# Half-precision Strassen sums with a power-of-two scale found on the chip, and one packed DRAM block per weight group

## The chip, the cores and the metric

The kernel runs on one core of one Trainium2 chip. The metric is device time in microseconds (us), the median of several executions. One execution of each kernel is also profiled; its trace gives the start, the duration and the releasing event of every instruction. TensorE is called PE, its weight loads PEld, VectorE DVE, ScalarE ACT, GpSimd POOL, SyncE SP. An engine name followed by q (ACTq, SPq, POOLq) is that engine's sequencer issuing a DMA.

Executions are fast or slow (over 1.5% above the fastest of the same kernel).

## The reference, cut to what matters

The input is 2048 tokens of width 1024 in bfloat16. The kernel does layernorm, linear attention with 32 heads, and a SwiGLU feed-forward block of width 3584:

```python
xn = layernorm(x)
s  = attention(xn, wqkv, wo)             # linear attention, phi(q), phi(k)
g  = silu((silu(xn @ w_gate) * (xn @ w_up)) @ w_down)
return x + s * g
```

The two large products `xn @ w_gate` and `xn @ w_up` are the subject. `w_gate` and `w_up` are 1024 x 3584 each.

## The kernel before

The kernel has these stages, in order: K and V projections; Q, attention and output projection (called "Q to S" below); the feed-forward block for one half of the tokens (gate/up, then down); and the same for the other half. I call the two gate/up stages pass 0 and pass 1.

Gate and up are computed by Strassen-Winograd. The weights are cut in 28 groups of 1024 x 256 (14 gate, 14 up). A group is a 2 x 2 block matrix; seven products of blocks replace eight. Three of them use the weights as they are, four use sums of weight blocks, T1 to T4, and of activation blocks, S1 to S4. Each product is four matmuls of 128x128 by 128x512, so a group is 28 matmuls. POOL makes the T sums once, in fp32, and keeps a copy in DRAM, which pass 1 (and part of pass 0) loads back:

```python
def t_pair():
    return [tp.tile([P, 2, HK, P], F32R, name="T%d" % k, tag="T") for k in range(2)]

def emit_T(key, w):
    b11, b12 = w[:, 0:HK, 0:P], w[:, 0:HK, P:2 * P]
    b21, b22 = w[:, HK:DC, 0:P], w[:, HK:DC, P:2 * P]
    ...
    nc.gpsimd.tensor_tensor(out=T1, in0=b12, in1=b11, op=ALU.subtract)
    nc.gpsimd.tensor_tensor(out=T2, in0=b22, in1=T1, op=ALU.subtract)
    nc.gpsimd.tensor_tensor(out=T3, in0=b22, in1=b12, op=ALU.subtract)
    nc.gpsimd.tensor_tensor(out=T4, in0=b21, in1=T2, op=ALU.subtract)
    ...   # first time: t_drams[g] <- ta, tb  (two fp32 tiles of 512 KB)

def emit_Ssum(p):
    ...
    S1, S2, S3, A22 = [sp.tile([P, HK, TB], F32R, ...) for k in range(4)]
    S4 = sp.tile([P, HK, TB], F16, name="S4", tag="S4")

def emit_a(key):           # four of the seven products of a group
    ...
    prod(y_[:], lambda k: T2[:, k, :], lambda k: S2[:, k, :], True)
    prod(x_[:], lambda k: w[:, k, 0:P], lambda k: x1[:, k, :], True)
    prod(zw[:, 0, :], lambda k: T3[:, k, :], lambda k: S3[:, k, :], True)
    prod(zw[:, 1, :], lambda k: T1[:, k, :], lambda k: S1[:, k, :], True)
    nc.scalar.copy(out=s1[:], in_=x_[:])                     # PSUM leaves through ACT and DVE
    nc.vector.tensor_tensor(out=s2[:], in0=y_[:], in1=s1[:], op=ALU.add)
```

Fourteen of the 28 groups are prepared during K/V and Q to S; the others arrive raw in pass 0 and are summed there. ACT both evicts PSUM for PE and issues DMAs.

## Time and profile before

The median is 803.16 us (802.13 to 803.51, three runs). First the page of the profiled execution of the kernel before, its engine line and its chain of work (what the end of the program depended on, followed back) as shares of the span:

```profile
PE 790.2 (99%) x3787; PEld 431.3 (54%) x3787; DVE 453.0 (57%) x739; ACT 232.9 (29%) x384; POOL 215.5 (27%) x357
...
PE 96%; DVE 2%; ACT 0%; DMA 0%; issue 0%; DVEq 0%; ACTq 0%
```

PE is busy for 99% of the 799.1 us span, and 96% of the chain is PE. So nothing else can be made faster with profit. The next lines are groups of PE instructions of the kernel before; the columns are line, engine, operation, output<-inputs, partitions x elements, type and count, then busy us and mean ns of one, then idle time before them:

```profile
L641 PE MATMUL zw<-S,T 128*128 128x512 f32 x672 | 175.3, 409 | 0.0
...
L641 PEld LDWEIGHTS zw<-S,T 128*128 128x128 f32 x672 | 126.4, 188 | 32.3
...
L641 PEld LDWEIGHTS <-w_sb 128*128 128x128 bf16 x672 | 56.8, 98 | 83.1 <-issue 30.5
```

A weight load of fp32 type takes 188 ns, one of 16-bit type 98 ns. The pitch of the groups shows in the timeline of PE (start, duration, what). Two neighbouring groups of pass 1 in the kernel before:

```profile
652.05 3.12 PE L641 MATMUL zw<-S,T 128*128 128x512 f32 x12
...
658.37 3.12 PE L641 MATMUL zw<-S,T 128*128 128x512 f32 x12
```

They start 6.32 us apart, 225.7 ns per matmul. Stages with only 16-bit matmuls run at 215.8 ns. That is the room the change aims at.

### The profile page before, as it was taken

Reading aid. Unit: us, or ns where it says so; the run is one execution under the profiler, and the core shown is the slowest. Engines: PE = TensorE matmul, PEld = TensorE weight load, DVE = VectorE, ACT = ScalarE, POOL = GpSimd, SP = SyncE. Lnnn points to the kernel's source line nnn. Section 1 sums busy time; section 2 is a strip of 40 time slices with the busy share of each in tenths; the row PEclk is TensorE's granted clock in tenths of the full one; section 3 lists DMA queues with packets and bytes.
Section 4 is the critical chain, followed back from the end, with each engine's and each line's share of the span. In section 5 each row is a group of like instructions: output and inputs, shape, how many; then the busy total and the mean of one; then the engine's idle time right before and its main releaser. Section 6 shows DMA issues by size and latency. Waiting matters only on the chain.

```text
span 799.1 us, 10159 instructions
## 1 busy us (share of the span) xinstructions
PE 790.2 (99%) x3787; PEld 431.3 (54%) x3787; DVE 453.0 (57%) x739; ACT 232.9 (29%) x384; POOL 215.5 (27%) x357
## 2 busy tenths in 40 slices
PE   8999999999999999999999999999999999999997
PEld 3544444554445666666664444466666666544443
DVE  7787344774575767677672071366767667601305
ACT  4544334866534222222220030122222232200102
POOL 0576799055005443535710020100000000000100
PEclk9999999999999999999999999999999999999999
DMA  9378974386478778787786457499777787744641
GB/s 321 114 175 172 300 260 187 103 207 191 133 168 275 235 244 266 230 270 232 224 304 218 151 188 284 129 324 310 239 251 253 256 251 251 253 169 137 232 131 53
DMA packets 155296, 173.68 MB, mean 217 GB/s; under 512 B 35440, under 2 KB 114672, under 8 KB 155248
## 3 DMA queue, kind: packets, MB, share of 16 engines
q1 hardware_dynamic: 143584, 136.20, 55.9%
q0 software_dynamic: 9216, 32.51, 11.5%
q10 hardware_dynamic: 2448, 4.33, 1.6%
q8 instruction: 30, 0.49, 0.2%
q14 instruction: 18, 0.15, 0.1%
HBM read 127.93 MB, written 37.75 MB: 207 GB/s over the span
## 4 chain that ended last, share of the span: by engine, by line
PE 96%; DVE 2%; ACT 0%; DMA 0%; issue 0%; DVEq 0%; ACTq 0%
PE zw L641 26%; PE kv_ps L402 13%; PE xb L641 12%; PE y_pd L726 12%; PE y_ps L726 11%; PE s_ps L578 7%; PE q_ps L158 7%; PE yb L641 7%; PE nd_ps L551 1%; PE kvz L424 1%; DVE sy L763 1%; DVE stats L321 0%; DVE io L764 0%; DMA xp<-in_A_x_dram 0%; PE tr_ps L386 0%
## 5 line engine op out<-in xcount | busy, mean ns | idle before, releaser
L641 PE MATMUL zw<-S,T 128*128 128x512 f32 x672 | 175.3, 409 | 0.0
L726 PEld LDWEIGHTS <-hT 128*128 128x128 bf16 x896 | 87.7, 98 | 105.7
L641 PEld LDWEIGHTS zw<-S,T 128*128 128x128 f32 x672 | 126.4, 188 | 32.3
L641 PE MATMUL xb<-xnT,w_sb 128*128 128x512 bf16 x448 | 115.2, 380 | 0.0
L402 PE MATMUL kv_ps<-wkv_sb,xnT 128*128 128x512 bf16 x512 | 113.6, 379 | 0.7 <-ACT r_t L139 0.5
L726 PE MATMUL y_ps<-w_sb,hT 128*128 128x512 bf16 x448 | 103.2, 379 | 0.0
L726 PE MATMUL y_pd<-w_sb,hT 128*128 128x512 bf16 x448 | 102.9, 379 | 0.0
L766 POOL DMA_DIRECT2D out_dram<-io x24 | 13.0, 540 | 332.6 <-DVE io L764 332.6
L641 PEld LDWEIGHTS <-w_sb 128*128 128x128 bf16 x672 | 56.8, 98 | 83.1 <-issue 30.5
L763 DVE TENSOR_TENSOR sy<-sy,io 128x512 f32<-128x512 f32 (+1 forms) x33 | 22.2, 672 | 137.6 <-ACT sy L762 137.4
L402 PEld LDWEIGHTS <-xnT 128*128 128x128 bf16 x512 | 49.3, 98 | 57.2 <-issue 0.7
L660 ACT COPY s<-xb 128x512 f32<-128x512 f32 x56 | 32.7, 584 | 158.4 <-PE xb L641 158.4
L214 POOL TENSOR_TENSOR T<-w_sb 128x512 fp32r<-128x512 bf16 x28 | 33.0, 1178 | 154.8 <-DMA w_sb<-in_B_w_up_dram 87.2
L661 DVE TENSOR_TENSOR s<-yb,s 128x512 f32<-128x512 f32 x56 | 38.6, 688 | 61.9 <-ACT s L660 61.9
L641 PE MATMUL yb<-S,T 128*128 128x512 f32 x224 | 71.5, 441 | 0.0
L158 PE MATMUL q_ps<-xnT,wq_sb 128*128 128x512 bf16 x256 | 58.2, 379 | 0.0
L698 ACT ACTIVATE sg<-sg 128x1024 f32<-128x1024 f32 x28 | 29.6, 1058 | 97.6 <-DVE sg L694 97.6
L641 PE MATMUL zw<-S,w_sb 128*128 128x512 f16 x224 | 58.0, 382 | 0.0
L578 PE MATMUL s_ps<-wo_sb,oT 128*128 128x512 bf16 x256 | 57.8, 379 | 0.0
L762 ACT ACTIVATE sy<-y_pd 128x512 f32<-128x512 f32 x16 | 8.7, 595 | 159.9 <-PE y_pd L726 159.9
L662 DVE TENSOR_TENSOR s<-zw,s 128x512 f32<-128x512 f32 x56 | 38.7, 692 | 26.6 <-PE zw L641 26.5
L704 DVE TENSOR_TENSOR hT<-cu,sg 128x1536 bf16<-128x1536 f32 x28 | 49.9, 1781 | 0.0
(84 smaller groups left out, 808.3 us busy)
## 6 DMA issues: line engine op xcount, KB each, us to landing
w_sb<-in_B_w_down_dram SPq DMA_DIRECT2D x56, 512.0 KB, 4.0
T<-t_g SPq DMA_DIRECT2D x52, 512.0 KB, 4.3
w_sb<-in_B_w_gate_dram SPq DMA_DIRECT2D x40, 512.0 KB, 4.8
t_g<-T POOLq DMA_DIRECT2D x28, 512.0 KB, 4.8
w_sb<-in_B_w_up_dram SPq DMA_DIRECT2D x28, 512.0 KB, 6.6
t_u<-T POOLq DMA_DIRECT2D x28, 512.0 KB, 4.8
T<-t_u SPq DMA_DIRECT2D x28, 512.0 KB, 4.8
s_dram<-s_sb ACTq DMA_DIRECT2D x16, 256.0 KB, 4.1
```

The costliest lines, as they stand in the source:

```text
L158: nc.tensor.matmul(q_ps[:], lhsT=wq_sb[:, dc, g * P:(g + 1) * P], rhs=xn_ap(dc, btok), start=(dc == 0), stop=(dc == DC - 1))
L214: nc.gpsimd.tensor_tensor(out=T1, in0=b12, in1=b11, op=ALU.subtract)
L402: mm = nc.tensor.matmul(kv_ps[:], lhsT=xn_ap(dc, tok), rhs=wkv_sb[:, dc, c * CW:(c + 1) * CW], start=(dc == 0), stop=(dc == DC - 1))
L578: mm = nc.tensor.matmul(s_ps[:], lhsT=oT[:, c, ttok], rhs=wo_sb[:, c, cc * CW:(cc + 1) * CW], start=(c == 0), stop=(c == G - 1))
L641: nc.tensor.matmul(out, lhsT=lhs(k), rhs=rhs(k), start=(first and k == 0), stop=(k == HK - 1), skip_group_check=True)
L660: nc.scalar.copy(out=s1[:], in_=x_[:])
L661: nc.vector.tensor_tensor(out=s2[:], in0=y_[:], in1=s1[:], op=ALU.add)
L662: nc.vector.tensor_tensor(out=s3[:], in0=zw[:, 0, :], in1=s2[:], op=ALU.add)
L698: nc.scalar.activation(out=c[:, 1:3, :], in_=c[:, 1:3, :], func=ACT.Silu)
L704: nc.vector.tensor_tensor(out=hv[:, TB:4 * TB], in0=c[:, 1:4, :].rearrange("p a b -> p (a b)"), in1=sg[:, 1:4, :].rearrange("p a b -> p (a ...
L726: nc.tensor.matmul(ys[(t, c)], lhsT=h[:, fc, tt], rhs=wt[:, o:o + CW], start=(fc == 0), stop=(fc == FC - 1), skip_group_check=True)
L763: nc.vector.tensor_tensor(out=sy[:], in0=sy[:], in1=s_in[:, cs], op=ALU.mult)
```

## The change

The intent is to make all gate/up matmuls 16-bit. Sums of weights in fp16 could overflow or underflow for other weights, so every group is first scaled by an exact power of two, found on the chip from the sum of the absolute weights; the inverse scale is applied where PSUM is evicted. Raw weights, scaled, and their four sums go into one 1 MB block per group, so that pass 1 loads one block. The core of the diff, with cuts:

```diff
-    wgu = ctx.enter_context(tc.tile_pool(name="wgu", bufs=3))
-    tp = ctx.enter_context(tc.tile_pool(name="tp", bufs=8))
+    wgu = ctx.enter_context(tc.tile_pool(name="wgu", bufs=NPK))      # 7 slots of 1 MB
+    stp = ctx.enter_context(tc.tile_pool(name="stp", bufs=4))
...
+    def emit_st0(key, t):
+        asum = stp.tile([P, 1], FP32, name="asum", tag="asum")
+        nc.scalar.activation(out=t[:, 1]..., in_=t[:, 0]..., func=ACT.Abs, accum_out=asum[:])
+        sd = dram.tile([P, 1], FP32, name="sd_%s%d" % key[1:])
+        nc.scalar.dma_start(out=sd[:], in_=asum[:])
+        st_tiles[key] = sd
+
+    def emit_st1(key):
+        sd = st_tiles.pop(key)
+        bc = stp.tile([P, P], FP32, name="bc", tag="bc")
+        nc.scalar.dma_start(out=bc[:], in_=sd[:].rearrange("p o -> (o p)").partition_broadcast(P))
+        st_tiles[key] = bc
+
+    def emit_st2(key, t):
+        bc = st_tiles.pop(key)
+        ...
+        nc.vector.tensor_reduce(out=tot[:], in_=bc[:], op=ALU.add, axis=mybir.AxisListType.X)
+        ...                                     # exponent of the total -> scale cs, inverse rc
+        nc.vector.tensor_scalar(out=w, in0=w, scalar1=cs_all[:, c:c + 1], scalar2=None, op0=ALU.mult)
...
     def emit_T(key, t):
...
+        pk = dram.tile([P, 2, DC, FW], BF16, name="pk_%s%d" % key[1:])
+        nc.gpsimd.dma_start(out=pk[:], in_=t[:])
...
-        emit_phi(phiw, q_ps[:], pqT[:, g, :], TB, in_place=True, act=b > 0 or g % 2 == 1)
+        emit_phi(phiw, q_ps[:], pqT[:, g, :], TB, in_place=True, act=b > 0)
...
-            nc.scalar.copy(out=s1[:], in_=x_[:])
-            nc.vector.tensor_tensor(out=s2[:], in0=y_[:], in1=s1[:], op=ALU.add)
+            nc.scalar.activation(out=s1[:], in_=x_[:], func=ACT.Copy, scale=rc)
+            nc.vector.scalar_tensor_tensor(out=s2[:], in0=y_[:], scalar=rc, in1=s1[:], op0=ALU.mult, op1=ALU.add)
...
-                io = tp.tile([P, 2, D], BF16, name="io", tag="T")
+                io = iop.tile([P, 2, D], BF16, name="io", tag="io")     # 2 buffers instead of 8
```

`asum` is one number per partition. To get the total onto all partitions, the change stores the 128 numbers to DRAM (128 rows of 4 bytes: 512 bytes in all) and loads them back as one row, broadcast to 128 partitions. I call this store and load the trip. `emit_st0`, `emit_st1` and `emit_st2` of one group run in three successive steps, so each engine has other work between them. In pass 0 a raw group is loaded six groups ahead, summed five ahead, scaled three ahead and used one ahead.

## The prediction

> **What bounds the kernel now.** TensorE. The page's engine table gives PE 790.2 us of a 799.1 us span, the chain of waits is 96% PE, and the list of PE's waits sums to about 4 us, all before 129 us. So time can only come from the pitch of the matmuls.
>
> **Pitch, from the PE timeline.** In the K/V, Q and down stages 32 bf16 matmuls start 6.90 us apart: 215.8 ns each (the Trainium skill, TensorE: Matmul & The Clock Gate, "Back-to-back issue gap", has about 216). In the gate/up stage each group of 28 matmuls takes 6.32 us: 225.7 ns each, the same in every group of both passes, so a rate and not a wait. 16 have fp32 operands; their weight loads take 188 ns against 98 ns for bf16 (groups by form). The same page ("Weight-path perf modes") says that fast weight load is off for FP32; the trace agrees with the factor of two.
>
> **What the change removes.** All gate/up matmuls become 16-bit. 784 matmuls per pass at 215.8 instead of 226 ns is 169.2 instead of 177.2 us: -8.0 us per pass, **-15.9 us** in all. This lies wholly on the critical path. Fewer bytes moved, faster Strassen sums and a bf16 hT product (1.78 to about 0.9 us) are off it and save nothing.
>
> **What it adds.** Per weight group (28, once each): a 2048-wide abs-sum on ACT (about 1.95 us), two small DMAs through DRAM (about 2 us each), five DVE operations (about 1.3 us). Where they bite:
> - Pass 0 of gate/up: ACT and DVE have room (DVE 120 us of 178). The chain for an unprepared group ends on POOL: scale done about 2.2 us after its predecessor's group, T1 and T2 2.4 us later, needed at 6.04 us. Slack about 1.4 us; the three raw groups at the end may cost some tenths. +0.5 us, and +0.5 at the start of the pass.
> - Q/attention stage (129 to 175 us): ACT was busy 15.6 of 18 us and DVE 15.9 of 18 us there. Q block 0 now goes wholly through DVE (two ops, 1.35 us per 1.73 us of PE) plus the mask products plus scaling, then block 1 wholly through ACT plus abs-sums. Summing durations in program order, DVE falls some 4 us behind and PE waits for PSUM: **+2.5 us** (1 to 5).
> - Tail: the output staging has 2 buffers instead of 8, so in the last sweep the loads of x and s for token tile 2 wait for tile 0's store. I expect **+2 us** (1 to 3.5) after the last matmul.
>
> **Predicted:** 803.2 - 15.9 + 1 + 2.5 + 2 = about **792 us** (-1.4%); 8 in 10 between 787.5 and 799. Faster by over 2%: 0.07; within 2%: 0.87; slower: 0.06.
>
> **What would show it.** Gate/up groups 6.04 us apart in both passes, weight loads 98 ns there; PE waits on DVE between 140 and 180 us; last matmul to end of span about 7 us instead of 5; no PE waits in the down stages or in pass 1.
>
> **What would make it wrong.** POOL slower on fp16 output or blocked by DVE: 14 unprepared groups, each with 1.4 us of slack, could give back up to 10 us. ACT stuck on a DMA semaphore in its fixed order, stopping evictions of PSUM, in the prep stretch (85 to 175 us). If all additions were hidden, 787.3 us, just on the 2% line.

## The result, and the profile after

The kernel became slower: 896.01 us (892.45 to 908.0, four runs, of which the one of 908.0 counts as slow and is left out of the ratio) against 802.64 us for the kernel before in the same session. Ratios in this document are the mean time of one kernel's fast runs over that of the other's of the same rounds, so they are not quite the ratio of the medians quoted; here it is 1.1149, with a 95% interval of 1.1121 to 1.1176.

The page of the changed kernel, the same two lines, and the chain by line:

```profile
PE 798.3 (89%) x3787; PEld 363.4 (41%) x3787; DVE 482.9 (54%) x883; ACT 283.8 (32%) x430; POOL 196.6 (22%) x329
...
PE 57%; DMA 23%; POOL 6%; DVE 5%; issue 4%; ACT 3%; ACTq 0%; SPq 0%; POOLq 0%; DVEq 0%
PE zw L681 14%; PE y_pd L777 11%; PE y_ps L777 10%; DMA sd_u<-asum 8%; PE xb L681 7%; PE s_ps L616 6%; DMA sd_g<-asum 6%; PE yb L681 4%; DMA bc<-sd_g 3%; PE q_ps L162 3%; DMA w_sb<-in_B_w_up_dram 3%; ACT w_sb L221 3%; POOL lnw L393 1%; POOL lnw L394 1%; POOL rstd L396 1%
```

No engine but PE is near its limit. PE is now idle for 11% of the span, and its busy time did not fall by the hoped-for 16 us either (more on that below). The chain is 23% DMA. Most of what it names are the half-kilobyte stores of the sums (`sd_g`, `sd_u`) and their broadcast loads (`bc`); a raw weight load has 3%.

The hoped-for gain is there where nothing disturbs it. In pass 1 two neighbouring groups of the changed kernel start 6.04 us apart, as predicted:

```profile
653.39 1.89 PE L681 MATMUL zw<-S,w_sb 128*128 128x512 f16 x8
...
659.43 1.89 PE L681 MATMUL zw<-S,w_sb 128*128 128x512 f16 x8
```

Stage lengths, from the starts of the first matmul of each stage in the timeline of PE (us; the last row is what follows the last matmul):

| stage | before | changed | difference |
|---|---|---|---|
| K/V, up to the first Q matmul | 128.7 | 168.5 | +39.8 |
| Q to S | 117.8 | 138.8 | +21.0 |
| pass 0 gate/up | 177.2 | 213.7 | +36.5 |
| down, pass 1, down | 370.5 | 363.3 | -7.2 |
| tail | 4.9 | 9.4 | +4.5 |
| span | 799.1 | 893.7 | +94.6 |

But for 4.5 us of the tail, the loss sits in the three stages in which groups are summed and scaled. These lines are picked from the list of waits of the changed kernel (engine, line, what ended the wait; us in total, times, longest). They are ACT's and DVE's largest waits for the two small DMAs, and PE waits of the same stages:

```profile
ACT s L702 <- DMA sd_u<-asum: 50.8, 6, 10.6
DVE tot L236 <- DMA bc<-sd_g: 46.5, 11, 10.5
...
DVE tot L236 <- DMA bc<-sd_u: 19.4, 7, 6.2
ACT v_sb L459 <- DMA sd_g<-asum: 17.1, 3, 6.4
...
PE kv_ps L444 <- DVE pk_sb L145: 14.8, 2, 13.1
PE kvz L466 <- ACT v_sb L459: 14.3, 4, 5.2
...
PE yb L681 <- POOL w_sb L252: 12.7, 7, 3.7
```

How one such wait reaches PE is best seen in the timeline. These lines are from the start of pass 0 (start, duration, engine, line, what; in brackets the idle time before it and what ended it):

```profile
311.79 0.33 ACTq L224 DMA_DIRECT2D sd_u<-asum  x1
...
322.02 0.33 ACTq L230 DMA_DIRECT2D bc<-sd_u  x1
322.39 0.69 ACT L702 ACTIVATE s<-xb,rc_all 128x512 f32<-128x512 f32 x1 [10.63 <-DMA sd_u<-asum]
...
323.11 0.75 DVE L703 SCALAR_TENSOR_TENSOR s<-yb,rc_all,s 128x512 f32<-128x512 f32 x1 [10.66 <-ACT s L702]
323.91 1.86 PE L681 MATMUL xb<-xnT,w_sb 128*128 128x512 bf16 x4 [6.13 <-DVE s L703]
326.75 3.34 PE L681 MATMUL zw<-S,w_sb 128*128 128x512 f16 x8 [0.97 <-DVE cg L742]
...
334.24 1.89 PE L681 MATMUL zw<-S,w_sb 128*128 128x512 f16 x8
```

ACT issues the store of one group at 311.79 us. The next thing in its queue is the broadcast of the same group, which may not be issued before the store has landed. It lands 10.2 us later. The eviction behind it (L702) had its input long before, but has to wait its turn. So DVE waits, PSUM is not freed, and PE stands still for 6.13 us.

The wait is not all. After it, eight matmuls take 3.34 us; eight of the same form take 1.89 us at 334.24 us. Between 322.9 and 329.7 us the granted TensorE clock is half (0.50 in that window). The trace of the changed kernel has eight PE waits over 3 us, and beside each lies such a half-clock stretch, of 3.4 to 13.7 us; the kernel before has neither until its tail. The span is 99.5 us longer than that of the same kernel without the trip (experiment 1, 794.2 us). About 78 us of this are PE's waits (86.0 against 8.0 us), and about 21 us are slower matmuls: PE is busy for 798.3 instead of 777.2 us with 3787 matmuls in both. In experiment 10, whose longest PE wait is 2.8 us, the clock stays full until the tail. That long waits bring the clock down fits all these traces, but no run tests it alone.

The DMA list of the changed kernel (what, issuing queue, count, size of one, median us from issue to landing) says how slow the trip is:

```profile
w_sb<-in_B_w_gate_dram SPq DMA_DIRECT2D x14, 512.0 KB, 8.6
w_sb<-in_B_w_up_dram SPq DMA_DIRECT2D x14, 512.0 KB, 10.7
...
bc<-sd_g ACTq DMA_DIRECT2D x14, 64.0 KB, 9.1
bc<-sd_u ACTq DMA_DIRECT2D x14, 64.0 KB, 6.2
...
sd_g<-asum ACTq DMA_DIRECT2D x14, 0.5 KB, 10.5
sd_u<-asum ACTq DMA_DIRECT2D x14, 0.5 KB, 10.4
```

A store of half a kilobyte takes as long as a load of 512 KB. And the raw weight loads are slow as well: 8.6 and 10.7 us, where the kernel before had 4.8 and 6.6.

### The profile page after: what moved, and what is told of

The parts are those of the page before. It is cut to its first block, busy times and chain, and to the rows that moved or that the text cites. A ratio compares the mean times of both kernels' runs of the same rounds, so it can differ in the third digit from the quotient of the medians.

```text
span 893.7 us, 10185 instructions
## 1 busy us (share of the span) xinstructions
PE 798.3 (89%) x3787; PEld 363.4 (41%) x3787; DVE 482.9 (54%) x883; ACT 283.8 (32%) x430; POOL 196.6 (22%) x329
## 4 chain that ended last, share of the span: by engine, by line
PE 57%; DMA 23%; POOL 6%; DVE 5%; issue 4%; ACT 3%; ACTq 0%; SPq 0%; POOLq 0%; DVEq 0%
PE zw L681 14%; PE y_pd L777 11%; PE y_ps L777 10%; DMA sd_u<-asum 8%; PE xb L681 7%; PE s_ps L616 6%; DMA sd_g<-asum 6%; PE yb L681 4%; DMA bc<-sd_g 3%; PE q_ps L162 3%; DMA w_sb<-in_B_w_up_dram 3%; ACT w_sb L221 3%; POOL lnw L393 1%; POOL lnw L394 1%; POOL rstd L396 1%
## 5 line engine op out<-in xcount | busy, mean ns | idle before, releaser
L681 PEld LDWEIGHTS <-w_sb 128*128 128x128 f16 (+1 forms) x1568 | 154.1, 99 | 228.9 <-issue 27.3
L681 PE MATMUL zw<-S,w_sb 128*128 128x512 f16 x672 | 165.3, 383 | 9.3 <-DVE cg L742 8.6
L251 POOL TENSOR_TENSOR w_sb<-w_sb 128x512 f16<-128x512 bf16 x28 | 32.1, 1145 | 282.1 <-DVE w_sb L244 166.4
L702 ACT ACTIVATE s<-xb,rc_all 128x512 f32<-128x512 f32 x56 | 38.2, 682 | 168.5 <-PE xb L681 93.6
L703 DVE SCALAR_TENSOR_TENSOR s<-yb,rc_all,s 128x512 f32<-128x512 f32 x56 | 42.0, 749 | 88.8 <-ACT s L702 88.8
L681 PE MATMUL yb<-S,w_sb 128*128 128x512 f16 x224 | 59.3, 388 | 19.6 <-POOL w_sb L252 12.7
L221 ACT ACTIVATE w_sb<-w_sb 128x2048 bf16<-128x2048 bf16 x28 | 53.4, 1906 | 31.0 <-DMA w_sb<-in_B_w_up_dram 11.0
L681 PE MATMUL zw<-xnT,w_sb 128*128 128x512 bf16 x224 | 57.5, 379 | 0.0
L748 ACT ACTIVATE sg<-cg 128x1024 bf16<-128x1024 f32 x28 | 29.5, 1055 | 63.3 <-DVE cg L742 63.3
L704 DVE SCALAR_TENSOR_TENSOR s<-zw,rc_all,s 128x512 f32<-128x512 f32 x56 | 42.0, 750 | 8.0 <-PE zw L681 4.2
## 6 DMA issues: line engine op xcount, KB each, us to landing
pk_g<-w_sb POOLq DMA_DIRECT2D x14, 1024.0 KB, 10.4
w_sb<-in_B_w_up_dram SPq DMA_DIRECT2D x14, 512.0 KB, 10.7
```

The source lines that it names most:

```text
L221: nc.scalar.activation(out=t[:, 1].rearrange("p a b -> p (a b)"), in_=t[:, 0].rearrange("p a b -> p (a b)"), func=ACT.Abs, accum_out=asum[:])
L681: nc.tensor.matmul(out, lhsT=lhs(k), rhs=rhs(k), start=(first and k == 0), stop=(k == HK - 1), skip_group_check=True)
L702: nc.scalar.activation(out=s1[:], in_=x_[:], func=ACT.Copy, scale=rc)
L703: nc.vector.scalar_tensor_tensor(out=s2[:], in0=y_[:], scalar=rc, in1=s1[:], op0=ALU.mult, op1=ALU.add)
L704: nc.vector.scalar_tensor_tensor(out=s3[:], in0=zw[:, 0, :], scalar=rc, in1=s2[:], op0=ALU.mult, op1=ALU.add)
L748: nc.scalar.activation(out=sg[:, 1:3, :], in_=cf[:], func=ACT.Silu)
```

## The experiments

Sixteen kernels ran; all gave correct results. "Expected" texts name runs by label: e1 to e4 are the runs of sections 1 to 4; e6, e7 and e10 of section 5; e8 of 6; e11 and e12 of 7; e5 and e9 of 8; e13 to e15 of 9; e16 of 10.

### 1. Is it the trip, the packs, or the added work?

Theory A: the trip through DRAM, waited for in the in-order queues. Rival B: the 1 MB packs crowd the DMA queues. Rival C: ACT and DVE have too much work. The first experiment takes away only the two small DMAs; abs-sums, scaling, packs and order all stay, and the scale comes from a constant tile:

```diff
-        sd = dram.tile([P, 1], FP32, name="sd_%s%d" % key[1:])
-        nc.scalar.dma_start(out=sd[:], in_=asum[:])
...
-        nc.scalar.dma_start(out=bc[:], in_=sd[:].rearrange("p o -> (o p)").partition_broadcast(P))
...
-        bc = st_tiles.pop(key)
+        bc = bc_const            # [P, P], filled with 100.0
```

> The changed kernel without the trip of the abs-sums through DRAM: the store of 128 sums, the broadcast load and all waits on them are gone; the DVE operations that turn a sum into a scale stay and read a constant tile instead (its exponent is the one that this data has), and the abs-sum stays on ACT. Theory A (ACT, which evicts PSUM in fixed order, stands still until a 10 us store has landed before it may issue the broadcast, and the whole chain of load, sum, store, broadcast, scale, T is longer than the look-ahead): about 792 to 798 us, PE waits under 10 us in all. Rival B (DMA congestion: 1 MB packs written and read back, loads that land after 9 to 11 us, slots that come free late): stays above 850 us. Rival C (ACT and DVE simply have too much to do with the sums and the scaling): stays above 850 us too.

Measured: 795.95 us, ratio 0.9908 (0.9892 to 0.9925). The stage lengths return: K/V 132.1, Q to S 120.3, pass 0 169.6 us. PE's waits sum to about 8 us. The raw loads land again in 4.3 and 5.0 us (list of DMAs of this run). B and C fall, as packs and work are all still there. Theory A holds so far, but this run takes away the waits and the traffic of the two small DMAs together.

### 2. Is the gain itself real?

The kernel before, with nothing changed but the types of the T and S sums:

```diff
-        return [tp.tile([P, 2, HK, P], F32R, name="T%d" % k, tag="T") for k in range(2)]
+        return [tp.tile([P, 2, HK, P], F16, name="T%d" % k, tag="T") for k in range(2)]
...
-        S1, S2, S3, A22 = [sp.tile([P, HK, TB], F32R, ...) for k in range(4)]
+        S1, S2, S3, A22 = [sp.tile([P, HK, TB], F16, ...) for k in range(4)]
```

> The kernel before with nothing changed but the type: T1 to T4, their copies in DRAM, S1 to S3 and the copy of a22 in fp16 instead of fp32 words; no scale, no packs, no new order. The step of the prediction that gave -15.9 us by the pitch of 16-bit matmuls alone: 786 to 789 us, gate/up groups 6.04 us apart in both passes. If the pitch is held by something else (PSUM evictions by DVE, say), it stays above 795 us.

Measured: 787.75 us, ratio 0.9808 (0.9793 to 0.9823): 15.4 us less than the 803.14 us of its own kernel before, where 15.9 was predicted for the pitch. It is the fastest kernel. It has no scale, so its fp16 sums are safe only for weights in a range like that of this input.

### 3. The same total without DRAM

A matmul with a matrix of ones sums over the partitions and leaves the total on all of them:

```diff
-        sd = dram.tile([P, 1], FP32, name="sd_%s%d" % key[1:])
-        nc.scalar.dma_start(out=sd[:], in_=asum[:])
...
+        ps = pool.tile([P, CW], FP32, name="st_ps", tag=tag)
+        nc.tensor.matmul(ps[:, 0:1], lhsT=ones[:], rhs=asum[:], start=True, stop=True)
```

> The changed kernel with the trip through DRAM replaced by one matmul of a 128x128 tile of ones with the 128 sums (one column) into PSUM, read by DVE; abs-sum and scaling as in the change, so that the scale is still found on chip. Theory A: like the kernel without the trip, 792 to 800 us. Rivals B and C: above 850 us.

Measured: 798.22 us, ratio 0.9938 (0.9923 to 0.9953). The scale is found on the chip as intended, at 2.3 us more than with no trip and no sum over partitions at all.

### 4. Another engine issues the broadcast

```diff
-        nc.scalar.dma_start(out=bc[:], in_=sd[:].rearrange("p o -> (o p)").partition_broadcast(P))
+        nc.gpsimd.dma_start(out=bc[:], in_=sd[:].rearrange("p o -> (o p)").partition_broadcast(P))
```

> The changed kernel with the broadcast load issued by POOL instead of ACT, so that ACT no longer stands before a store that has not landed; DVE still waits for the broadcast. If ACT's place in the queue is all (A1), about 800 us. If the chain is also longer than the look-ahead (A2), DVE and POOL wait instead and only part comes back: 830 to 880 us.

Measured: 911.98 us in a single execution, outside everything expected. It is no better than the changed kernel; that it is worse is not shown, as one execution of that kernel took 908.0 us. The wait moved to POOL, whose queue also holds the T sums and the pack stores. The waits that a landing of `sd` ended there sum to 101 us, but 71.4 of them are one idle stretch around the start of pass 0, far longer than any store. PE then waited 42.9 us for POOL's sums. So moving the wait to another queue did not help; that the trip is too long for its look-ahead, whoever waits, is the reading that fits.

### 5. Two steps at the ends: the tail and the engine mix

The last sweep gets back room for x and s, in two weight slots that are free by then (experiment 1 plus this):

```diff
-                io = iop.tile([P, 2, D], BF16, name="io", tag="io")
-                xres, s_in = io[:, 0, :], io[:, 1, :]
+                if last:
+                    if t % 2 == 0:
+                        io4 = w_slot()[:].rearrange("p h a b -> p (h a b)").rearrange("p (k n) -> p k n", k=4)
+                    xres, s_in = io4[:, 2 * (t % 2), :], io4[:, 2 * (t % 2) + 1, :]
```

> The kernel without the trip, with x and s of the last sweep loaded into two free weight slots instead of the two staging buffers, so that no load there waits for a store. If the two staging buffers cost the tail 4.0 us (8.9 us from the last matmul to the end, 4.9 before), 792 us and a tail near 4.9 us. If the tail is long for another reason (order of the queue of SyncE), 796 us.

Measured: 792.81 us (ratio 0.9859, 0.9833 to 0.9886), tail 4.7 instead of 8.9 us. The two staging buffers cost about 4 us of tail, by a wait in the last sweep (3.1 us between the two medians).

Then the sum by matmul, with this tail and with the old mix of engines in Q block 0:

```diff
-        emit_phi(phiw, q_ps[:], pqT[:, g, :], TB, in_place=True, act=b > 0)
+        emit_phi(phiw, q_ps[:], pqT[:, g, :], TB, in_place=True, act=b > 0 or g % 2 == 1)
```

> Sum by a matmul with ones, the tail as in the run before it, and the evictions of Q block 0 shared between DVE and ACT in turn as in the kernel before. From 798.2: -4.0 by the tail, -2.3 by the Q stage, so 792 us, with no wait of PE between 135 and 250 us. If the Q stage's 2.3 us come from the sums and not from the eviction of block 0, 794 us.

Measured: 796.04 us (0.9903, 0.9873 to 0.9933), a miss: the tail gain came, but Q to S grew from 120.7 to 123.6 us. To tell whether the mix did that, the same without it:

> The kernel of e3_pe_sum (sum over partitions by a matmul with ones in place of the trip through DRAM, the scale still found on the chip) with the last sweep's x and s in two free weight slots, and with the engine mix of block 0 left as the changed kernel has it. If the tail and the mix act by themselves, as e6 and e7 say: 798.2 minus 4.2 is 794.0 us (793 to 795.5), the tail 4.7 us, the Q to S stretch 120.7 us as in e3 and so about 2 us faster than e7. If the longer Q to S stretch of e7 was the spread of the start and not the mix, this one has no reason to beat e7 and comes at 796.

Measured: 792.86 us (0.987, 0.9853 to 0.9886), Q to S 120.7 us, tail 4.7 us. So beside the abs-sums the new mix is the better one. In the profiled execution with the old mix, 1.4 of the 2.9 us are one more wait of PE for DVE, and 1.5 us a half-clock stretch right after it (16 Q matmuls in 5.13 us; 16 take 3.6 us elsewhere). The run without the old mix is the best version here that still finds its scale on the chip.

### 6. More time between the steps of the preparation

```diff
-                if i >= 8 and c % 2 == 1:
-                    k = 2 * (i - 8) + c // 2
-                    prep(2 * (k + 1) // 3 - 2 * k // 3)
+                if i >= 8 and c == 3:
+                    prep(1)
...
-            if g % 3 == 1:
+            if g == 4:
                 prep(1)
```

> The changed kernel, trip and all, with the preparation steps further apart (one per token tile in K/V instead of two in three half tiles, one in Q, then two per block), 7.4 us and more instead of 3.7 to 7.4. Theory A1 (ACT and DVE stand in their queues before a trip of two times 7 to 10 us that the next step comes too early for): K/V to S, which took 307 us against 247 before, comes back by most of the 60 us, to 255 to 270 us; pass 0, where the same trip must fit into five groups, stays about 210 us long instead of 169: about 845 to 860 us in all. If the loss in K/V to S has another cause, it stays above 295 us.

Measured: 893.94 us in a single execution, a miss. K/V gave back 26 of its 36 us over experiment 1 (142.8 us), but Q to S grew to 149.9 and pass 0 to 227.6 us. Steps moved into Q to S brought the same waits there, and ACT now also waited 15.0 us for raw weights, whose loads took 10.0 and 10.9 us in the median. So spacing alone was not the answer, and the slow loads needed a reason.

### 7. Do the losses of the stages add up?

Two kernels take the trip in one half and the matmul with ones in the other:

```diff
+    def trip(key):
+        return (key in raw_keys) == TRIP_IN_PASS_0     # False in one kernel, True in the other
```

> The changed kernel with the trip through DRAM kept for the 14 groups prepared ahead of the first pass, and the sum by a matmul with ones (as in e3) for the 14 groups of the first pass. If the trip costs where it stands, and the losses of the stages simply add: the changed kernel's 896.0 minus the 43.0 us by which its first pass was longer than that of e3 (213.7 against 170.7), so about 853 us (848 to 858); first weight of Q at 165 to 170 us, Q to S 136 to 141 us, the first pass 169 to 174 us. If the first pass is slow because the packs and stores of the prepared groups come late or the trip's queue is still in arrears there, the first pass stays over 180 us and the whole over 862.

> The mirror of it: the sum by a matmul with ones in the prep, the trip through DRAM only for the 14 groups of the first pass. If the losses add: e3's 798.2 plus 43.0, so about 841 us (836 to 846); K/V until 132 us and Q to S 121 us as in e3, the first pass 211 to 217 us. If the first pass of the changed kernel was slow only because it inherited delay from the prep, it comes under 190 us and the whole under 820.

Measured: 854.08 us with the trip in the preparation, as expected, and pass 0 was 170.7 us. So pass 0 inherits no delay from the trip of the preparation. (The split of the preparation was not as expected: K/V 164.5 us and Q to S 145.2 us.) With the trip in pass 0 only: 869.36 us, a miss by 28 us. K/V and Q to S were as short as in experiment 3, but pass 0 took 242.7 us instead of 213.7. The broadcasts landed there in 8.9 us in the median (5.8 in pass 0 of the changed kernel), and DVE waited 46.4 us for them (19.4). What the trip costs is therefore not a fixed number per group: it depends on how long its transfers take at that moment.

### 8. What makes the trip slow? First two probes

Experiment 1 with stores that nothing waits for, from the ACT queue, of three forms in turn (128 rows of 4 bytes, 16 rows of 4 bytes, 128 rows of 512 bytes):

```diff
+        if kind == "n128":
+            d = dram.tile([P, 1], FP32, ...)
+            nc.scalar.dma_start(out=d[:], in_=src[:, 0:1])
+        elif kind == "n16":
+            d = dram.tile([16, 1], FP32, ...)
+            nc.scalar.dma_start(out=d[:], in_=src[0:16, 0:1])
+        else:
+            d = dram.tile([P, P], FP32, ...)
+            nc.scalar.dma_start(out=d[:], in_=src[:, 0:P])
```

> The kernel without the trip, with DMAs from ACT that nothing waits for: at the place of each store, in turn a store of 128 rows of 4 bytes (what the change stores), of 16 rows of 4 bytes, and of 128 rows of 512 bytes; the same in pass 1 and in the down sweeps. Asks why half a kilobyte needs 10 us. If each row waits its turn behind the big transfers on its DMA engine (Q1), 16 rows land in 3 to 5 us, and 128 rows in about 10 us whether they hold 4 or 512 bytes, less where the DMA is less busy. If 4-byte writes are slow in themselves (Q2), 128 rows of 512 bytes land much sooner than 128 of 4. If it is a fixed cost of a DMA from ACT (Q3), all three take 10 us. The time of the kernel should stay at 796 to 802 us: the traffic costs nothing, only the waits do.

Measured: 810.28 us, a miss: stores that nobody waits for cost 14 us. Medians to landing in the preparation were 11.0, 10.4 and 7.5 us, in pass 1 10.3, 8.7 and 5.8 us. So rows of 4 bytes are slower than rows of 512 bytes with 128 times the data, though the forms share a queue here and can slow each other. ACT waited 23 us for raw weights in this run; these loads landed in 7.8 and 6.9 us (4.3 and 5.0 without the probe). The loss lay in Q to S (128.3 us, 8.0 more than in experiment 1) and in pass 1 (176.3 us, 7.1 more).

The second probe put four forms into pass 1 only:

```diff
+        if kind == "adj":                                   # 128 x 4 bytes next to each other
+            d = dram.tile([P, 1], FP32, ...);  nc.scalar.dma_start(out=d[:], in_=src[:, 0:1])
+        elif kind == "own":                                 # each in its own 512-byte block
+            d = dram.tile([P, P], FP32, ...);  nc.scalar.dma_start(out=d[:, 0:1], in_=src[:, 0:1])
+        elif kind == "w128":                                # 128 x 512 bytes
+            d = dram.tile([P, P], FP32, ...);  nc.scalar.dma_start(out=d[:], in_=src[:, 0:P])
+        else:                                               # one row of 512 bytes
+            d = dram.tile([1, P], FP32, ...);  nc.scalar.dma_start(out=d[:], in_=src[0:1, 0:P])
```

> The kernel of e1_no_trip, with one store that nothing waits for per group of the second pass, from the ScalarE queue: in turn 128 rows of 4 bytes next to each other, 128 rows of 4 bytes each in its own 512-byte block, 128 rows of 512 bytes, and one row of 512 bytes; seven of each. No abs-sums or other small DMAs run in that pass. If rows under 512 bytes are slow because they fall into the same 512 bytes and must follow one another, the adjacent rows stay at 8 to 11 us and the rows in their own blocks come to within 1.5 us of the full rows (about 6 us). If a row under 512 bytes is slow wherever it lies, both 4-byte forms stay within 1.5 us of each other, 2 us or more over the full rows. If the number of rows counts and not their bytes, all three forms of 128 rows are alike; in the first probe they were not (10.3 against 5.8 us in this pass). The single row tells the floor: 2 to 4 us if one row is cheap. Whole kernel: 796 to 800 us, if the 14 us that the first probe lost came from its probes ahead of the second pass; 805 or more, if those of the second pass cost it.

Measured: 795.31 us, so probes in pass 1 at this rate cost nothing: one store in four has adjacent 4-byte rows, where the first probe had two in three. Medians: adjacent 8.9, own block 7.5, full rows 4.9 us; for the single row the profile shows no landing. By the criterion this said "short rows are slow wherever they lie". That reading was wrong: the forms stood in one queue and slowed each other. The 1 MB reloads of that pass gave it away; they took 6.7 and 8.4 us, against 4.8 and 4.9 in experiment 1.

### 9. One form at a time

One form alone, 28 times, beside the same reloads in pass 1.

```diff
-        kind = ("adj", "own", "w128", "one")[k % 4]
+        kind = "adj"            # "own" and "w128" in the other two kernels
```

> e1_no_trip with one un-awaited store of 128 adjacent 4-byte rows per group of the second pass. Own landing 8 to 11 us, as in the other probes. If short rows slow the neighbours, the 1 MB reloads of that pass take 7 us or more (4.8 and 4.9 without probes). If only the large rows (which move 128 times the bytes) did it, they stay under 5.5. Whole kernel 795 to 797, as nothing waits there.

> The same with each 4-byte row in its own 512-byte block. If the shared block is what makes the short rows slow, own landing under 6.5 us and reloads faster than with adjacent rows by 1 us or more; if the shortness itself, own landing within 1.5 us of the adjacent ones and reloads alike.

> The same with 128 full rows of 512 bytes, 64 KB a store. If any other transfer of 128 rows slows the reloads, they take about as long as beside the short rows (7 us or more). If the shortness matters, own landing about 5 to 6 us and the reloads at 4.8 to 5.8 us.

The DMA list of each run, cut to 424 to 690 us, which holds pass 1 but for its last 8 us in the first of the three runs (median us from issue to landing at the end of a line). Adjacent 4-byte rows, 807.84 us in all:

```profile
w_sb<-pk_g SPq DMA_DIRECT2D x14, 1024.0 KB, 24.1
w_sb<-pk_u SPq DMA_DIRECT2D x14, 1024.0 KB, 25.5
...
adjacent128x4B<-bc_const ACTq DMA_DIRECT2D x26, 0.5 KB, 22.6
```

The same 4-byte rows, each in its own 512-byte block, 795.39 us in all:

```profile
w_sb<-pk_g SPq DMA_DIRECT2D x14, 1024.0 KB, 4.8
w_sb<-pk_u SPq DMA_DIRECT2D x14, 1024.0 KB, 4.9
...
ownblock128x4B<-bc_const ACTq DMA_DIRECT2D x28, 0.5 KB, 3.6
```

Full rows, 796.29 us in all:

```profile
w_sb<-pk_g SPq DMA_DIRECT2D x14, 1024.0 KB, 5.0
w_sb<-pk_u SPq DMA_DIRECT2D x14, 1024.0 KB, 4.9
...
full128x512B<-bc_const ACTq DMA_DIRECT2D x28, 64.0 KB, 3.7
```

The first two differ only in where the rows lie: same count, same bytes, same queue. Lying next to each other makes the stores land six times later (22.6 against 3.6 us) and the 1 MB reloads beside them five times later (24.1 against 4.8 us). These are times from issue to landing, with the wait behind earlier transfers in them, and not rates: from 551 to 688 us the reloads landed one per 6.9 us, while PE needs one per 6.04 us, so a queue built up. That run is 12.4 us longer than the one with the spread rows, all of it from pass 1 on, with PE waiting for the reloads, although nothing waited for the stores themselves. The granted clocks of the two executions, 0.997 and 0.996, show no sign of a slow state. So the shared block is what matters, by the criterion for the second of the three. The queue list of the same views says where the time went: the recorded 4-byte packets themselves took 1.1% of the time of the 16 DMA engines with adjacent rows and 0.9% with spread rows, but the packets of SP's queue, which holds the reloads, took 76.7% against 53.3%. The landing of 8 to 11 us and the total of 795 to 797 us expected for the adjacent rows were both too low: stores at this rate pile up.

### 10. The changed kernel with another form of store

The decisive run keeps the whole chain of waits and changes the form of the store to 128 full rows. Column 0 holds the sum, the rest a constant 80, and row 0 is broadcast:

```diff
-        asum = stp.tile([P, 1], FP32, name="asum", tag="asum")
+        asum = rows[n_rows[0] % 4]                  # four tiles [P, P], filled once with 80.0
+        n_rows[0] += 1
...
-                             func=ACT.Abs, accum_out=asum[:])
-        sd = dram.tile([P, 1], FP32, name="sd_%s%d" % key[1:])
+                             func=ACT.Abs, accum_out=asum[:, 0:1])
+        sd = dram.tile([P, P], FP32, name="sd_%s%d" % key[1:])
...
-        nc.scalar.dma_start(out=bc[:], in_=sd[:].rearrange("p o -> (o p)").partition_broadcast(P))
+        nc.scalar.dma_start(out=bc[:], in_=sd[0, :].partition_broadcast(P))
```

> The changed kernel with the same trip and the same waits, but the store as 128 full rows of 512 bytes (column 0 holds the sum, the other columns a constant 80), and the broadcast from row 0 of it, 512 bytes as before. The scale is then a power of two found from partition 0 alone and constants: a stand-in for the sum, on purpose, but exact, so the result stays correct. If the adjacent 4-byte rows are the cost (slow in landing, and slowing the loads): store 3.5 to 6 us, broadcast 3 to 6 us, raw loads back at 4.3 to 6 us, K/V 132 to 138 us, the first pass 170 to 178 us, the whole 798 to 815 us. If a trip of any form costs because ScalarE and VectorE wait for it in order, stores of 5 us instead of 10 save about half: 835 to 860 us.

Measured: 810.32 us (806.74 to 813.61), ratio 1.0105 (1.0074 to 1.0135). The DMA list of this run, to be held against that of the changed kernel above:

```profile
w_sb<-in_B_w_gate_dram SPq DMA_DIRECT2D x14, 512.0 KB, 6.6
w_sb<-in_B_w_up_dram SPq DMA_DIRECT2D x14, 512.0 KB, 4.7
...
sd_g<-asum ACTq DMA_DIRECT2D x14, 64.0 KB, 2.6
bc<-sd_g ACTq DMA_DIRECT2D x14, 64.0 KB, 4.2
sd_u<-asum ACTq DMA_DIRECT2D x14, 64.0 KB, 4.4
bc<-sd_u ACTq DMA_DIRECT2D x14, 64.0 KB, 2.9
```

The stores move 128 times the bytes and land in a quarter to less than half of the time. The broadcast, which is the same 64 KB load in both kernels, is faster too, and so are the raw loads. ACT's and DVE's waits shrank with them:

```profile
DVE tot L241 <- DMA bc<-sd_g: 12.4, 5, 5.0
...
ACT s L707 <- DMA sd_u<-asum: 3.9, 1, 3.9
```

Of the 100 us between the changed kernel (896.0) and the one without a trip (796.0), 85.7 us hang on the form of this store, and 14.4 us remain for having a trip at all, with waits in in-order queues. Stage by stage (us, profiled executions; that of the full-row trip is the fastest of its four, at 806.74 us):

| stage | changed | full-row trip | no trip | before in fp16 |
|---|---|---|---|---|
| K/V | 168.5 | 136.7 | 132.1 | 131.2 |
| Q to S | 138.8 | 125.4 | 120.3 | 118.0 |
| pass 0 gate/up | 213.7 | 171.4 | 169.6 | 169.2 |
| down, pass 1, down | 363.3 | 363.3 | 363.3 | 362.8 |
| tail | 9.4 | 8.1 | 8.9 | 4.9 |
| span | 893.7 | 804.9 | 794.2 | 786.1 |

This variant is an experiment and not a replacement: its scale is a power of two and exact, but it is found from partition 0 and constants.

## Why the prediction was right or wrong, point by point

- **What bounds the kernel before: right.** PE, at its pitch. The Trainium skill (TensorE: Matmul & The Clock Gate, "Weight-path perf modes") says that fast weight load needs a type other than FP32. The trace agrees: 188 ns in fp32, 98 to 99 ns in 16 bits.
- **-15.9 us from the pitch: right.** Groups are 6.04 us apart in pass 1 of the changed kernel, and experiment 2, which has the types alone, gained 15.4 us.
- **"two small DMAs through DRAM (about 2 us each)": this is the term that failed.** The store took 10.4 us and the broadcast 6.2 to 9.1 us in the median. About 2 us is what the Trainium skill (DMA: Bandwidth & Descriptors, "Anatomy of one DMA") gives as the fixed cost of a transfer that GpSimd issues; the prediction names no source for its figure. No store so small was in the trace of before to check it with (the smallest there, 64 KB, landed in 1.6 us); full rows came near it (2.6 to 4.4 us), the store of the change did not. The prediction did not ask where the rows lie. That this also slows the large transfers beside it was in nobody's sum, nor were the half-clock stretches beside PE's waits.
- **Pass 0, "+0.5 us, and +0.5 at the start": wrong by that term.** It became 213.7 us instead of 170. The slack argument took POOL as the end of the chain and let scaling start on time. By the measured medians the chain of a raw group is 10.7 (load) + 2.1 (abs-sum with its read-out) + 10.4 (store) + 6.2 (broadcast) + 1.5 (DVE) + about 2.3 (the first two sums on POOL), 33 us, against 30 us of look-ahead, which is five groups of 6.04 us. With the durations of experiment 10 (4.7, 4.4 and 2.9 us for load, store and broadcast) it is 18 us, and pass 0 was 171.4 us. These two sums are estimates from the measured parts.
- **The preparation stretch: the risk was named and not priced.** "ACT stuck on a DMA semaphore in its fixed order" is what the timeline shows. It was given as something that could go wrong, with no number, and it was 39.8 us in K/V alone, 36.4 more than without the trip.
- **Q/attention, +2.5 us: the size was right without the trip, by luck as far as these runs show.** Without the trip, Q to S is 2.3 us longer than with the fp16 types alone, and PE does wait for DVE there, as forecast (1.8 us in two waits for `o_blk`, near 154 and 163 us). But the cause given, Q block 0 wholly on DVE, is not supported: taking that back made Q to S 2.9 us longer (runs e7 and e10 of section 5 differ in nothing else). Why DVE is late there is open. With the trip the stage lost 21.0 us.
- **Tail, +2 us: the mechanism was right, the size low.** It is 4 us (8.9 us without the trip, 4.9 before), and the use of two free weight slots as buffers took all of it back.
- **The range.** The upper end, 799 us, allowed for engine work alone. The no-trip kernel, at 796.0 us, lies inside it, 4 us above the 792 predicted: about 2 us of that are the tail, and K/V, for which nothing was added, is 3.4 us longer than in the trace of before.

The cause, then: the 128 sums of a group lie side by side in 512 bytes of DRAM, and a store of such rows lands late and delays its neighbours. This is shown, by experiments 9 and 10. Two steps are argued and not shown. First, that the slow store comes from read-modify-write of one shared block: the Trainium skill (DMA: Bandwidth & Descriptors, "Specifications") says that transfers under 512 bytes do read-modify-write, and writes that share a block would then have to follow one another. The trace agrees only in part: rows of 4 bytes in their own blocks are as fast as full rows (3.6 against 3.7 us), so being short is not enough. The page of each run counts 106.95 MB read from HBM with adjacent rows, with spread rows and without a probe, so it shows no extra reads; whether it would count them is not known. Second, why the 1 MB transfers of another queue suffer: the same page ("Issuing engines are not separate DMA queues") says that DMAs of all engines run on the same 16 DMA engines, and the reloads issued by SP indeed landed after 24.1 instead of 4.8 us beside stores issued by ACT.

Also open: why the trip in pass 0 alone (the second run of experiment 7) was slower still than in the changed kernel; why the first 130 us are 2 to 4 us longer in the variants without a trip there, the fp16 one included (part may be spread: the profiled execution of the kernel before, 799.1 us, is the shortest, its others span 799.5 to 803.4 us); and how far apart rows must lie, as only 4 and 512 bytes were tried.

## What to carry to other kernels

Before you send a handful of per-partition numbers through DRAM, ask where the rows land: 128 rows of 4 bytes side by side cost far more than 128 full rows, and they delayed the large loads beside them, so look at the landing times of the large DMAs too. A sum over partitions by a matmul with ones needs no DRAM and cost about 2 us in the whole kernel. Put a DMA that must wait for another DMA in the queue of an engine that evicts PSUM only where the measured landing time fits the look-ahead. When PE waits for microseconds, look at the granted clock after the wait as well: here about a fifth of the loss was slower matmuls. And when you probe a form of transfer, probe it alone.

## What the Trainium skill lacked or had wrong

- DMA: Bandwidth & Descriptors, "Specifications" and "Why small descriptors are slow": they treat short transfers by size alone. The runs show that position decides: 128 rows of 4 bytes landed in 22.6 us when adjacent and in 3.6 us when each had its own 512-byte block.
- The same page, "Rules for kernel authors" ("Many small transfers: Coalesce into one large transfer"): it lacks the case in which many short rows of one DMA are packed into one 512-byte block of DRAM. There the packed form is the slow one, and 1 MB transfers of another queue beside it landed after 24.1 instead of 4.8 us. For stores to DRAM no page that I read names this effect on neighbours; the same page names one for remote DMA only.
- The same page, "Anatomy of one DMA": the fixed cost of about 2 us, which is given for the GpSimd path, is a poor estimate for a dependent small store issued by ACT in a busy kernel. The runs show 2.6 to 4.4 us for full rows and 10.4 us for the adjacent 4-byte rows.
- TensorE: Matmul & The Clock Gate, "Back-to-back issue gap": it gives about 131 ns as the sustained spacing of pairs of weight load and matmul at N=512, and about 216 ns as the isolated gap, which is the figure that the prediction quotes. Here 16-bit matmuls with a weight load each ran at 215.8 ns in every undisturbed stretch, 784 of them in a row in pass 1.
